# Moving the gates of a fused kernel out of its first twelve steps and spreading the conversion of its weights more evenly

## The chip, the cores and the metric

The kernel runs on one core of one Trainium2 chip. The metric is the device time of one execution in microseconds (us). Before the change the median is 494.94 us over four runs (490.22 to 495.63). All times inside a trace are microseconds from the start of its span; a timed run is about 1.8 us longer than its span.

## The reference

Two blocks follow each other. A gated linear attention recurrence runs over 768 positions of 4 × 8 heads of 48 values. Its output, laid out as 3072 rows of 384, goes through a multiplicative feed-forward network.

```python
# q, k, v, alpha: (4, 8, 768, 48) float32
for t in range(S):
    state = alpha[:, :, t, :, None] * state + np.einsum('bhd,bhe->bhde', k[:, :, t], v[:, :, t])
    y[:, :, t] = np.einsum('bhd,bhde->bhe', q[:, :, t], state)
x = y.transpose(0, 2, 1, 3).reshape(3072, 384)
a = x @ w1            # 384 x 1024
b = x @ w2
h = a * b @ w3        # 1024 x 1024
out = h @ w_out       # 1024 x 384
```

The four weights arrive as float64. The chip reads them as pairs of 32-bit words and converts them itself.

## The kernel before

The 3072 positions are cut into N = 24 chunks of 128; three chunks form one of eight groups. The kernel has three parts.

- **Part 1** is a loop over the chunks that does the recurrence; I call one pass a step. A step loads alpha, k, q and v a few chunks ahead (192 KB each, in rows of 48 floats), computes scores, a state and the result of the chunk before, and stores that result for its group.
- **Gates** are the products x @ w1 and x @ w2 of one group and one 128-column tile. They are done to full float32 accuracy in three parts. Half a gate, nine matmuls, is a *piece*. Pieces of the first groups are strewn into part 1 to fill TensorE's pauses.
- **Conversion** turns the raw 64-bit weights into three float32r parts. Each of the 12 tiles of w1 and w2 takes four *conversion steps*, which call VectorE and ScalarE; tiles are loaded up to three ahead.

Part 2 does the remaining gates, the conversion of w_out and w3 and eight folds w3 @ w_out. The final projection follows, 24 chunks.

```python
LATE = 10      # from this chunk on, the decays' sum uses two fp32r matmuls in place of one fp32

def convert(steps, ahead=3):
    for _ in range(steps):
        while weights and len(begun) < ahead:
            begun.append(weights.popleft())
            next(begun[-1])                       # issues the load of the raw tile
        if not begun:
            return
        ...                                       # one more step of the oldest tile

def load_gates(kk, c0, n):
    w = yield from to_fp32(None, ...)             # load; then 2 ScalarE, 5 VectorE instructions in 2 steps
    ...
    nc.scalar.activation(h, w, AF.Copy, ...)
    yield
    nc.vector.scalar_tensor_tensor(l, ...)
    nc.vector.scalar_tensor_tensor(m, ...)
```

The loop of part 1, with the places where gates and conversions are called:

```python
    convert(1, 1)                                 # ahead of the loop
    ...
    begin = {4 + 4 * g: (g, range(FH if g < 4 else KF)) for g in range(5)}

    for n in range(N + 1):
        store()                                   # the chunk's result, two transfers
        load_v(n + AHEAD - 1)
        load_a(n + 5)
        load_kq(n + AHEAD)
        if n:
            attend_state(n - 1)                   # L358
        if n < N:
            scores(n)                             # L339
        transposed(n + 1)                         # L299
        if n - 2 in begin:
            g, tiles = begin[n - 2]
            split_x(g, 0)                         # L385 to L387
            fill.extend(gate(g, f) for f in tiles)
        pieces = (0, 3, 3, 2)[(n - 6) % 4] if n > 5 else 0
        ...
        early = n < 7
        convert(1, 2 if n == 0 else 3)
        advance(n)
        if n:
            attend(n - 1)                         # L364
        outer(n)                                  # L311
        run(pieces > 0)                           # one piece
        if early:
            convert(1)
        decayed(n + 2)                            # L277: k and q times the decays
        logs(n + 4)                               # L246: logarithm of alpha
        if n in begin:
            load_x(begin[n][0])
        convert(early and n > 2)
        run(pieces > 1)
        decays(n + 3)                             # L261, or L264 from LATE on
        convert(early or n % 3 == 0)
        run(pieces > 2)
    store()
    ...
    todo, order = list(fill), []                  # part 2
    visits = [(g, range(FH, KF)) for g in range(4)] + [(g, range(KF)) for g in range(len(begin), NG)]
```

## Time and profile before

| view of the profile | value before | how to read it |
|---|---|---|
| span | 492.8 us | first to last instruction of the profiled run |
| PE (TensorE) busy | 462.0 us, 94% | nearly the whole span; ends of matmuls are modelled |
| DVE (VectorE) busy | 371.0 us, 75% | an average over stages with very different limits |
| ACT (ScalarE) busy | 250.1 us, 51% | |
| DMA queue q1 | 62.7% of 16 engines' span | again an average |
| chain that ended last | PE 73%, DVE 9%, DMA 8% | shares of the span |

The averages say that TensorE is the bound.

### The profile page before, as it was taken

To read this page: it belongs to the slowest core of one execution; us is meant where nothing else is said; L and a number is where in the kernel's file an instruction comes from. 1 tells how busy PE (TensorE), PEld (TensorE's weight loads), DVE (VectorE), ACT (ScalarE), POOL (GpSimd) and SP (SyncE) were. 2 spreads that over 40 slices of the span, in tenths; PEclk is the share of its full clock that TensorE was granted. 3 is DMA by queue.
4 is the path that set the end of the run, shared out by engine and by line. 5 is a ranking of instruction groups with operands and counts; after the bars stand their busy time and mean duration, and the time that the engine had idled before them with its cause. 6 is when DMAs were issued, how large, how long until landed. Compare 5 with 4: busy or idle time off the path is not lost.

```text
span 492.8 us, 9909 instructions
## 1 busy us (share of the span) xinstructions
PE 462.0 (94%) x3760; PEld 422.5 (86%) x3760; DVE 371.0 (75%) x620; ACT 250.1 (51%) x479; POOL 37.5 (8%) x83
## 2 busy tenths in 40 slices
PE   3788689999998979999999999999999999999997
PEld 1566479888998968999999988888888999999996
DVE  2779899887988684999999769686433786667771
ACT  2767677676765563555556444444222533333330
POOL 2132132021103100000000000000000000000000
PEclk9989999999999998999999999999999999999999
DMA  9999999899999963666454433320001875555511
GB/s 176 185 200 205 236 199 201 217 183 234 194 227 189 214 207 101 175 183 195 158 195 155 156 117 118 118 92 32 33 32 61 229 225 176 177 176 178 176 49 48
DMA packets 160495, 79.10 MB, mean 161 GB/s; under 512 B 104640, under 2 KB 154304, under 8 KB 160448
## 3 DMA queue, kind: packets, MB, share of 16 engines
q1 hardware_dynamic: 159168, 78.40, 62.7%
q0 software_dynamic: 1280, 0.08, 0.4%
q8 instruction: 29, 0.48, 0.4%
q14 instruction: 18, 0.15, 0.1%
HBM read 56.40 MB, written 22.06 MB: 159 GB/s over the span
## 4 chain that ended last, share of the span: by engine, by line
PE 73%; DVE 9%; DMA 8%; SPq 4%; issue 3%; ACT 2%; POOL 0%; DVEq 0%; POOLq 0%; ACTq 0%
PE bank L396 37%; PE bank L400 18%; PE bank L445 8%; DMA raw<-in_moe_w_dram 3%; PE bank L339 2%; PE bank L364 2%; DVE ms L342 2%; PE bank L439 1%; DMA xT<-xd 1%; DMA abd<-ab 1%; DMA dec<-ends 1%; PE bank L299 1%; SPq L130 1%; DVE qk L277 1%; SPq L124 1%
## 5 line engine op out<-in xcount | busy, mean ns | idle before, releaser
L396 PE MATMUL bank<-x,w 128*128 128x384 f32 x768 | 159.3, 341 | 0.0
L396 PEld LDWEIGHTS bank<-x,w 128*128 128x128 f32 x768 | 134.6, 188 | 3.5 <-issue 0.5
L398 ACT ACTIVATE t<-bank 128x384 f32<-128x384 f32 x152 | 74.5, 492 | 109.7 <-PE bank L396 97.8
L401 DVE SCALAR_TENSOR_TENSOR r<-bank,t 128x384 f32<-128x384 f32 x128 | 69.7, 555 | 34.0 <-ACT t L398 32.1
L400 PE MATMUL bank<-x,w 128*128 128x384 f32 x384 | 87.3, 335 | 0.4 <-DVE x L387 0.4
L396 PE MATMUL bank<-w3o,ab 128*128 128x384 f32 x384 | 70.4, 334 | 0.0
L400 PEld LDWEIGHTS bank<-x,w 128*128 128x128 f32 x384 | 68.3, 188 | 0.7 <-issue 0.7
L396 PEld LDWEIGHTS bank<-w3o,ab 128*128 128x128 f32 x384 | 66.9, 188 | 0.0
L445 PE MATMUL bank<-wo,w3T 128*128 128x384 f32 x128 | 42.6, 486 | 0.0
L189 ACT ACTIVATE rest<-raw 128x512 f32<-128x512 uint32 (+1 forms) x36 | 23.4, 651 | 33.0 <-DMA raw<-in_moe_w_dram 20.5
L412 DVE TENSOR_TENSOR ab<-r 128x384 f32<-128x384 f32 x64 | 35.6, 556 | 2.3 <-DMA abd<-ab 1.5
L400 PE MATMUL bank<-w3o,ab 128*128 128x384 f32 x192 | 37.1, 334 | 0.0
L445 PEld LDWEIGHTS bank<-wo,w3T 128*128 128x128 f32 x128 | 24.2, 189 | 14.9
L464 DVE TENSOR_TENSOR ab<-abl,ab 128x1024 fp32r<-128x1024 f32 x24 | 29.4, 1224 | 9.2 <-ACT ab L463 9.2
L339 PEld LDWEIGHTS bank<-qkT 48*128 48x128 f32 x384 | 25.4, 200 | 12.4 <-ACT qkT L301 5.7
L339 PE MATMUL bank<-qkT 48*128 48x128 f32 x384 | 30.3, 299 | 6.0 <-ACT qkT L301 4.3
L463 ACT ACTIVATE ab<-abl 128x1024 fp32r<-128x1024 f32 x24 | 25.5, 1064 | 19.0 <-PE bank L400 18.8
L400 PEld LDWEIGHTS bank<-w3o,ab 128*128 128x128 f32 x192 | 33.6, 188 | 0.0
L342 DVE TENSOR_TENSOR ms<-bank,keep 128x512 int32<-128x512 int32 x48 | 31.1, 684 | 1.7 <-PE bank L339 1.7
L194 ACT ACTIVATE power<-power,rebias 128x512 uint32<-128x512 uint32 (+1 forms) x36 | 25.3, 705 | 12.2 <-DVE power L193 12.2
L401 DVE SCALAR_TENSOR_TENSOR o<-bank,t 128x384 f32<-128x384 f32 x24 | 13.4, 557 | 22.4 <-issue 13.7
L277 DVE TENSOR_TENSOR qk<-kq,e 128x768 f32<-128x768 f32 x24 | 22.9, 953 | 9.5 <-ACT e L268 7.2
(69 smaller groups left out, 540.1 us busy)
## 6 DMA issues: line engine op xcount, KB each, us to landing
abd<-ab SPq DMA_DIRECT2D x64, 192.0 KB, 2.7
abl<-abd SPq DMA_DIRECT2D x24, 512.0 KB, 4.5
raw<-in_moe_w_dram SPq DMA_DIRECT2D x16, 512.0 KB, 3.9
xT<-xd SPq DMA_DIRECT2D x12, 576.0 KB, 4.2
raw<-in_moe_w_dram SPq DMA_DIRECT2D x24, 256.0 KB, 4.8
ac<-in_alpha_dram SPq DMA_DIRECT2D x24, 192.0 KB, 5.0
kq<-in_k_dram SPq DMA_DIRECT2D x24, 192.0 KB, 5.4
kq<-in_q_dram SPq DMA_DIRECT2D x24, 192.0 KB, 4.3
```

Of the source, the lines that this page charges most:

```text
L194: nc.scalar.activation(power, power, AF.Relu, scale=2.0 ** 23, bias=rebias)
L277: nc.vector.tensor_mul(qks[n % 3][:, :, :, 0:D], st.pop(("kq", n)), st.pop(("e", n)).rearrange("p i (h d) -> p i h d", h=H))
L339: nc.tensor.matmul(sc[i][:, j, :], qkT[r, 0, j, :], qkT[r, 1, j, :], start=True, stop=True)
L342: nc.vector.tensor_tensor(ms[:, i].bitcast(I32), sc[i].bitcast(I32), keep_bc, op=ALU.bitwise_and)
L396: nc.tensor.matmul(p1, w[part][i], x[part][i], start=(part == i == 0), stop=(part == 1 and i == n - 1))
L398: nc.scalar.activation(t, p1, AF.Copy, scale=(1.0 + 1.0 / P) * scale)
L400: nc.tensor.matmul(p2, w[2][i], x[2][i], start=(i == 0), stop=(i == n - 1))
L401: nc.vector.scalar_tensor_tensor(to, p2, -scale, t, op0=ALU.mult, op1=ALU.add)
L412: nc.vector.tensor_mul(ab, *r)
L445: nc.tensor.matmul(po, w3T[:, j, :], wo[:, j, :], start=(j == 0), stop=(j == KF - 1))
L463: nc.scalar.activation(t[:, 0], ab, AF.Copy, scale=1.0 - 2.0 ** -13)
L464: nc.vector.tensor_sub(t[:, 1], ab, t[:, 0].bitcast(FP32))
```

## The change

The intent: the first twelve steps lose their gates, and every step calls two conversion steps, so that VectorE and TensorE have less to do early on and the steps get shorter. At most two weight tiles are under way, not three. The eleven pieces that had been strewn there go to part 2. From step 12 on the same 24 pieces as before are done, now those of the groups 0 to 2; x of group 3 is only split, in step 24.

```diff
-    LATE = 10
+    LATE = 16
...
-    convert(1, 1)
...
-    begin = {4 + 4 * g: (g, range(FH if g < 4 else KF)) for g in range(5)}
+    begin = {10 + 4 * g: (g, range(FH if g < 3 else KF)) for g in range(4)}
...
-        pieces = (0, 3, 3, 2)[(n - 6) % 4] if n > 5 else 0
+        pieces = (0, 3, 3, 2)[n % 4] if n >= 12 else 0
...
-        early = n < 7
-        convert(1, 2 if n == 0 else 3)
+        convert(1, 2)
...
-        if early:
-            convert(1)
+        convert(1, 2)
...
-        convert(early and n > 2)
...
-        convert(early or n % 3 == 0)
...
-    visits = [(g, range(FH, KF)) for g in range(4)] + [(g, range(KF)) for g in range(len(begin), NG)]
+    visits = [(g, range(FH, KF)) for g in range(3)] + [(g, range(KF)) for g in range(len(begin), NG)]
```

Before step 12 this makes 24 conversion steps where there were 32, one of them ahead of the loop. "Halved" below means the first seven steps: 14 conversion steps where there were 25 in the loop. Steps 7 to 11 have more than before, 10 where there were 6.

## The prediction

> **What bounds the kernel now.** I read the 40 slices first, to see which engine is full where; then the busy time stage by stage; then the order of time of TensorE and of the SP queue, to price single pieces. Times are microseconds from the span's start. The slices:
>
> ```profile
> PE   3788689999998979999999999999999999999997
> DVE  2779899887988684999999769686433786667771
> PEclk9989999999999998999999999999999999999999
> DMA  9999999899999963666454433320001875555511
> ```
>
> One slice is 12.3 us. TensorE is full from the sixth slice on, but for the slice near 185; before that VectorE and the DMA engines are the full ones, and the DMA engines stay full until about 185, where the part with the recurrence (part 1) ends. I found the borders of the steps from the score matmuls (L339, one burst per step): step 0 starts at 15.1, step 7 at 58.0, step 12 at 100.3, and the last recurrence matmuls (L364, chunk 23) end at 195.5. The busy time of these stages:
>
> ```profile
> core 0: us, PE busy (x) PEld busy (x) DVE busy (x) ACT busy (x) POOL busy (x), PEclk, DMA share, GB/s
> 15.00:58.00 43.00, 35.26 (x512) 27.90 (x512) 36.53 (x64) 30.02 (x65) 10.23 (x20) 0.92 1.05 201
> 58.00:100.30 42.30, 39.37 (x495) 35.25 (x494) 39.91 (x69) 30.12 (x65) 9.29 (x14) 1.00 0.98 213
> 100.30:195.50 95.20, 89.35 (x1131) 81.34 (x1131) 72.75 (x126) 57.35 (x129) 14.47 (x30) 0.98 0.87 196
> 195.50:389.30 193.80, 193.80 (x1033) 176.53 (x1032) 148.81 (x280) 92.18 (x169) 0.00 (x0) 1.00 0.39 125
> 389.30:492.80 103.50, 99.83 (x576) 99.50 (x575) 68.95 (x73) 35.24 (x46) 0.00 (x0) 1.00 0.51 154
> ```
>
> Rows: steps 0 to 6, which have no gates; steps 7 to 11, with gates; the rest of part 1; gates and folds alone; the final projection. TensorE never pauses in the fourth row. So anything moved there costs its whole TensorE time, and anything gained must come from the 30 us or so in which TensorE waits in the first three rows and before them.
>
> Two prices from the order of time, TensorE first, then the SP queue at the start, when nothing but input loads is under way:
>
> ```profile
> 198.68 1.20 PE L396 MATMUL bank<-x,w 128*128 128x384 f32 x6
> 199.72 0.68 PE L400 MATMUL bank<-x,w 128*128 128x384 f32 x3
> 200.24 1.03 PE L396 MATMUL bank<-x,w 128*128 128x384 f32 x5
> ...
> 2.68 0.87 SPq L124 DMA_DIRECT2D ac<-in_alpha_dram  x1
> 3.60 0.83 SPq L136 DMA_DIRECT2D v<-in_v_dram  x1
> 4.47 0.92 SPq L130 DMA_DIRECT2D kq<-in_k_dram  x1
> 5.43 1.00 SPq L131 DMA_DIRECT2D kq<-in_q_dram  x1
> 6.48 1.10 SPq L124 DMA_DIRECT2D ac<-in_alpha_dram  x1
> 7.62 1.49 SPq L181 DMA_DIRECT2D raw<-in_moe_w_dram  x2
> ```
>
> Half a gate (nine matmuls, one "piece") takes 200.24 - 198.68 = 1.56. A 192 KB load of alpha, k, q or v takes the queue about 0.94 (mean of the five), one weight tile in two halves about 1.5; the two stores of a chunk's result took 0.86 (later in the same view). I take these issue times as the rate at which the full DMA engines accept work.
>
> **What the Trainium skill says.** "Trace Analysis", Identifying the Most-Contended Engine: matmul busy time is a poor measure, as matmuls are pipelined. The trace agrees: one gate matmul is shown with a mean of 341 ns, but nine take 1.56, 173 ns each; I count by pitch. "DMA: Bandwidth & Descriptors", Specifications: runs of 512 B or more are needed for line rate. A row of a head here is 48 floats, 192 B, and the trace fits: 201 GB/s at a share of 1.05 in part 1, but 229 GB/s at a share of only eight tenths in the slice near 388 that loads 512 B rows. "TensorE: Matmul & The Clock Gate", Part 1, puts the clock at half after an idle window. The trace agrees: after TensorE stood 2.16 for the state of step 3, sixteen L364 matmuls took 1.90 at 35.9 and 1.02 at 41.9. The same page (Architectural detail) says that VectorE and ScalarE are strict FIFOs; so a conversion that stands ahead of a mask delays it:
>
> ```profile
> 181.41 0.44 PE L358 MATMUL bank<-qkT,T 48*64 48x128 f32 x4
> 183.29 0.65 PE L358 MATMUL bank<-qkT,T 48*64 48x128 f32 x12 [1.45 <-DVE ms L342]
> ```
>
> Here the mask stood behind a split of x (L386, 1.35).
>
> **The change, part by part.**
>
> *Gates moved.* Before, pieces run in the pattern 0, 3, 3, 2 from step 6 to step 24: 3+3+2+0+3 = 11 before step 12, 24 in steps 12 to 23, 3 in step 24. After: none before step 12, 8+8+8 = 24 in steps 12 to 23, none in step 24. The gates and folds after part 1 then take, before, 93 pieces (3, and 45 gates) x 1.56 = 145.1, plus eight folds of 6.06 (12.30 from fold to fold less two gates) = 48.5: 193.6, which is the 193.8 of the fourth row. After: 52 gates = 104 pieces x 1.56 = 162.2, plus 48.5 = 210.7. That is +17.2, all of it on the path. The projection stays at 103.5. So the new span is E + 210.7 + 103.5 = E + 314.2, where E is the end of part 1, and it breaks even with 492.8 at E = 178.6: part 1 has to give 16.9 of its 195.5.
>
> *Conversions halved.* One weight takes four convert steps and, by pitch, about 3.7 of VectorE (two at 0.34, five at 0.60). Before: 26 convert steps in steps 0 to 6, 0.93 weight a step, so 3.4 of VectorE, beside 2.34 for the recurrence itself (two masks at 0.60, decay product 0.87, state 0.27): 5.8 against the 6.1 that such a step lasted. After: two convert steps a step, 1.84, sum 4.2. VectorE stops being the bound of the early steps. TensorE needs 4.5 (steps 1 and 4 lasted that: 21.44 to 25.95, 40.28 to 44.78).
>
> *DMA in the early steps.* A step asks for four loads (3.8), two stores (0.86) and half a weight (0.75): 5.4, more than TensorE or VectorE. So the DMA engines set these steps. For the scores of step 12, what was issued up to about step 9 must have landed: 54 loads x 0.94 = 50.8, eight chunks' stores 6.9, seven weights 10.5; 68.2 from about 3.0, so 71 at the earliest. The same count for step 7 of the kernel before is 34 loads, three stores, seven weights = 45.1, due at 48, while step 7 came at 58.0: a stretch of 55.0/45.1 = 1.22. With that stretch step 12 comes at 86. I choose half of the stretch, 1.13, and 80: a part of it came from weight loads that stood in the SP queue for buffers VectorE had still to read, and with two weights under way and three raw buffers this goes. So 20 us of the 100.3, of which 17.2 are the moved pieces and some 3 a true gain.
>
> *LATE from 10 to 16.* Six chunks lose a ScalarE copy (0.51) and a VectorE subtraction (0.56), and trade two matmuls of 0.17 for an fp32 one of 0.85: about 3 us of TensorE in all, in steps that the DMA engines bound, so hidden.
>
> *Steps 12 to 24.* The same 24 pieces, so 95.2 as before, plus what the delayed conversions do: 24 convert steps where there were 16, 8 x 0.92 = 7.4 of VectorE, which goes from 72.75 to some 80 of 95. A split (about 2.55) falls in steps without pieces, in which VectorE then has 2.34 + 1.84 + 0.47 + 2.55 = 7.2 against TensorE's 4.3. Waits for the mask, 0.9 to 1.5 long, already stand at three of these steps; each grows by some 0.6. With step 24's split ahead of its first gate I put the sum at 3.
>
> *One xT load and split less* (11 for 12), outside the tight stages: nothing.
>
> Sum: E = 80 + 95.2 + 3 = 178.2; span 178.2 + 314.2 = 492.4 against 492.8. A timed run is 1.8 longer than the span (494.63 for 492.8): 494.2.
>
> **Rivals.** (1) *VectorE alone bounds the early steps.* Then they fall to TensorE's 4.5 to 4.7, step 12 starts at 15 + 12 x 4.7 = 71, and the time is 485. For it: VectorE is the full row between 36 and 84, and two early steps did last 4.5. Against it: the DMA share is about 1 there as well, and those two steps drew on loads already made. (2) *DMA bounds all of part 1.* The bytes hardly fall (seven ab stores and one xT load less), step 12 comes at 86 or later, steps 12 to 24 hold more weight loads, and the moved pieces are nearly pure loss: 499 to 506. For it: the share of 0.87 in the third row. Against: TensorE is busy for 89 of 95 there. (3) *VectorE becomes the bound in steps 12 to 24*, with conversions, gates and splits together: 5 to 8 more, about 500.
>
> **Range and chances.** The rivals lie at 485 and 506 on both sides of a central case that nearly cancels, so the 2% limits (485 and 505) need a rival in full. 486 to 503; faster 0.08, same 0.80, slower 0.12.
>
> **What would show it.** Right: step 12's scores at 78 to 84; a DMA share near 1 and VectorE at some seven tenths before it; part 1 ending near 178; 211 between that and the projection, with TensorE unbroken. Wrong: step 12 before 75 (the DMA floor is no floor) or after 87; part 1's second half much longer than 98, with TensorE waiting for masks; half-clock stretches of more than 7 us in the early steps.

## The result, and the profile after

| | runs | median us | range |
|---|---|---|---|
| before | 4 | 494.94 | 490.22 to 495.63 |
| after | 4 | 509.27 | 506.57 to 511.57 |

The ratio is 1.031, with a 95% interval of 1.023 to 1.039: slower. A ratio here is the mean time of one kernel's fast runs over the mean of the other's fast runs of the same rounds, so it is not quite the ratio of the medians. The prediction was 494.2, with a range of 486 to 503; the time lies above it.

The slices of the kernel after; one slice is 12.6 us:

```profile
PE   3978686899899999999999999999999999999997
DVE  2498666678988989999997677873349467777761
PEclk9989899779899999999999999999999999999999
DMA  9999999999997555656552253200057235655511
```

VectorE's slices from the fifth to the eighth fell from 8 or 9 tenths to 6, as intended. The DMA engines are still full there. TensorE's clock, which the kernel before held at nine tenths, falls to seven at the eighth and ninth slice.

The stages of the kernel after, cut at the scores of step 12, at the end of the last recurrence matmuls and at the projection. The columns are those of the same view in the prediction (the stage and its length, busy time of each engine with its instructions, clock, share of the DMA engines, GB/s):

```profile
13.06:88.62 75.56, 60.89 (x906) 47.31 (x906) 53.23 (x89) 46.56 (x103) 19.63 (x34) 0.91 1.06 195
88.62:187.20 98.58, 93.73 (x1134) 84.60 (x1130) 82.05 (x145) 62.12 (x136) 17.85 (x30) 0.93 0.86 200
187.20:401.30 214.10, 211.89 (x1132) 193.66 (x1131) 165.39 (x304) 97.99 (x182) 0.00 (x0) 1.00 0.42 131
401.30:504.80 103.50, 99.75 (x576) 99.43 (x574) 64.11 (x68) 34.12 (x45) 0.00 (x0) 1.00 0.44 135
```

In the first stage no engine is full: TensorE 60.9 of 75.6, VectorE 53.2. Only the share of the DMA engines is at 1. Side by side with the kernel before and with what the prediction said:

| us | before | after | change | predicted after |
|---|---|---|---|---|
| scores of step 0 at | 15.1 | 13.1 | −2.0 | |
| scores of step 12 at | 100.3 | 88.6 | −11.7 | 80 |
| from there to the end of part 1 | 95.2 | 98.6 | +3.4 | 98.2 |
| from there to the projection | 193.8 | 214.1 | +20.3 | 210.7 |
| projection | 103.5 | 103.5 | 0 | 103.5 |
| span | 492.8 | 504.8 | +12.0 | 492.4 |

The last column misses by 8.6, 0.4 and 3.4. Most of the 3.4 shows in TensorE's order of time at the start of part 2 (start, duration, engine, line, and in brackets how long it was idle before and what it waited for):

```profile
187.65 0.79 PE L396 MATMUL bank<-x,w 128*128 128x384 f32 x3 [0.42 <-ACT x L385]
189.14 0.79 PE L396 MATMUL bank<-x,w 128*128 128x384 f32 x3 [0.69 <-DVE x L386]
190.50 0.76 PE L400 MATMUL bank<-x,w 128*128 128x384 f32 x3 [0.57 <-DVE x L387]
```

Part 2 now begins with a group whose split has only just been issued, in step 24. Its first gate waits for the three instructions of the split one after another. The second half of that gate begins at 191.10, 3.9 after the end of part 1; at its full pitch, 1.56, it would have begun at 188.8. That is 2.3 of the 3.4; the other 1.1 is spread over the part. In the kernel before, the last split of part 1 was issued in step 22 (VectorE's part began at 181.28), so that x was ready for the pieces at the start of part 2.

In the first stage TensorE waits, and the matmuls after a wait are slow as well:

```profile
58.87 1.65 PE L261 MATMUL bank<-la,after 128*128 128x384 f32 x2 [3.54 <-ACT la L246]
60.45 1.13 PE L358 MATMUL bank<-qkT,T 48*64 48x128 f32 x16
61.51 2.08 PE L339 MATMUL bank<-qkT 48*128 48x128 f32 x16
63.38 1.06 PE L299 MATMUL bank<-ident,qk 64*128 64x64 f32 x16
```

The sum of the decays waits 3.54 for the logarithm of alpha. The matmuls after it run at half rate: the scores take 2.08, where they take 1.16 later on. Summed from the start to 110 us (the longest stands ahead of step 0), the waits of TensorE for this logarithm (in total, how often, the longest) are in the kernel after

```profile
PE bank L261 <- ACT la L246: 14.3, 6, 4.5
```

and in the kernel before

```profile
PE bank L261 <- ACT la L246: 8.6, 4, 4.3
```

This suggested to me at first that alpha comes too late in the queue. The experiments tell otherwise.

### The profile page after: what moved, and what is told of

The parts are those of the page before. It is cut to its first block, busy times and chain, and to the rows that moved or that the text cites.

```text
span 504.8 us, 9918 instructions
## 1 busy us (share of the span) xinstructions
PE 470.6 (93%) x3760; PEld 427.0 (85%) x3760; DVE 367.4 (73%) x612; ACT 245.4 (49%) x472; POOL 41.0 (8%) x83
## 4 chain that ended last, share of the span: by engine, by line
PE 56%; DVE 3%; DMA 2%; issue 1%; ACT 0%; DVEq 0%; ACTq 0%
PE bank L396 32%; PE bank L400 16%; PE bank L445 6%; DMA raw<-in_moe_w_dram 2%; PE bank L439 1%; DVE r L401 1%; DVE w L199 0%; DVE ab L412 0%; DVE power L193 0%; DVE power L197 0%; DVE x L387 0%; DVE mant L196 0%; ACT t L398 0%; ACT rest L189 0%; DVE mant L190 0%
## 5 line engine op out<-in xcount | busy, mean ns | idle before, releaser
L396 PE MATMUL bank<-x,w 128*128 128x384 f32 x768 | 161.3, 344 | 3.4 <-ACT x L385 2.3
L396 PEld LDWEIGHTS bank<-x,w 128*128 128x128 f32 x768 | 136.2, 191 | 7.7 <-ACT x L385 2.7
L398 ACT ACTIVATE t<-bank 128x384 f32<-128x384 f32 x152 | 74.1, 491 | 119.1 <-PE bank L396 104.7
L400 PE MATMUL bank<-x,w 128*128 128x384 f32 x384 | 88.5, 338 | 0.8 <-DVE x L387 0.6
L400 PEld LDWEIGHTS bank<-x,w 128*128 128x128 f32 x384 | 69.0, 190 | 1.9 <-PE bank L396 1.4
L189 ACT ACTIVATE rest<-raw 128x512 f32<-128x512 uint32 (+1 forms) x36 | 23.3, 650 | 31.0 <-DMA raw<-in_moe_w_dram 25.6
L400 PE MATMUL bank<-w3o,ab 128*128 128x384 f32 x192 | 37.1, 334 | 0.0
L463 ACT ACTIVATE ab<-abl 128x1024 fp32r<-128x1024 f32 x24 | 25.5, 1062 | 18.8 <-PE bank L400 18.8
L301 ACT COPY qkT<-bank 128x512 f32<-128x512 f32 x48 | 26.0, 586 | 17.3 <-PE bank L299 17.3
L339 PEld LDWEIGHTS bank<-qkT 48*128 48x128 f32 x384 | 26.5, 210 | 7.5 <-ACT qkT L301 2.3
L401 DVE SCALAR_TENSOR_TENSOR o<-bank,t 128x384 f32<-128x384 f32 x24 | 13.4, 558 | 26.2 <-issue 15.2
```

The source lines that it names most:

```text
L301: nc.scalar.copy(qkT[:, :, :, ds(DP * half, DP)], tp[half])
L339: nc.tensor.matmul(sc[i][:, j, :], qkT[r, 0, j, :], qkT[r, 1, j, :], start=True, stop=True)
L396: nc.tensor.matmul(p1, w[part][i], x[part][i], start=(part == i == 0), stop=(part == 1 and i == n - 1))
L398: nc.scalar.activation(t, p1, AF.Copy, scale=(1.0 + 1.0 / P) * scale)
L400: nc.tensor.matmul(p2, w[2][i], x[2][i], start=(i == 0), stop=(i == n - 1))
L401: nc.vector.scalar_tensor_tensor(to, p2, -scale, t, op0=ALU.mult, op1=ALU.add)
```

## The experiments

The theories under test were these.

- **A, arrival.** The transfers together set the first twelve steps, with the gates or without them.
- **L, lateness of alpha.** Not their sum but their order: alpha, or the logarithm that is made of it, comes too late, and TensorE waits for it.
- **C, conversion.** The conversion's instructions stand ahead of the recurrence's own on VectorE and ScalarE; in one form of this theory, ahead of the logarithm. The expectations also name a wider form **V**: VectorE and ScalarE, with the conversions, set these steps.

Each kernel of the table was profiled and timed in three rounds against the kernel before on the same chip; the exception is the loads alone, which had one look. "To 12" is from the scores of step 0 to those of step 12, "second half" from there to the end of part 1, "rest" from there to the projection. "Wrong" marks kernels that give a wrong result on purpose. All runs were fast ones but one of e13. The ratios of e5, e13 and e18 leave out the first, profiled run; this matters for e13 alone.

| kernel | to 12 | second half | rest | span | ratio to before (95%) |
|---|---|---|---|---|---|
| before | 85.2 | 95.2 | 193.8 | 492.8 | 1 |
| after | 75.6 | 98.6 | 214.1 | 504.8 | 1.031 (1.023 to 1.039) |
| e1: before, gates moved alone | 86.2 | 92.1 | 212.4 | 509.1 | 1.039 (1.034 to 1.044) |
| e2: after, LATE = 10 | 78.9 | 98.0 | 213.3 | 506.8 | 1.037 (1.031 to 1.042) |
| e3: after without loads of v (wrong) | 64.0 | 96.0 | 212.1 | 488.6 | 0.994 (0.989 to 1.000) |
| e4: after, alpha one step earlier | 76.5 | 106.6 | 212.7 | 512.3 | 1.039 (1.032 to 1.046) |
| e5: before without loads of v (wrong) | 85.8 | 94.7 | 193.9 | 493.6 | 1.012 (1.007 to 1.016) |
| e7: after, conversions without loads (wrong) | 66.2 | 88.6 | 212.8 | 485.9 | 0.994 (0.990 to 0.998) |
| e8: after, loads without conversions (wrong) | 69.0 | 93.1 | 214.6 | 492.4 | 1.010 (1.005 to 1.015) |
| e9: e4 and the logarithm earlier | 74.1 | 104.2 | 213.7 | 508.5 | 1.040 (1.036 to 1.044) |
| e11: gates from step 8 on | 89.7 | 86.6 | 200.1 | 493.0 | 1.004 (1.000 to 1.009) |
| e13: after with useless matmuls | 80.4 | 90.3 | 212.4 | 499.8 | 1.030 (1.023 to 1.036), with a slow run; see below |
| e15: before without the first conversion | 92.3 | 92.0 | 193.8 | 494.4 | 1.000 (0.994 to 1.007) |
| e16: before, loads without conversions (wrong) | 84.1 | 91.9 | 193.7 | 485.3 | 0.987 (0.982 to 0.993) |
| e17: e1 without loads of v (wrong) | 74.3 | 94.2 | 212.2 | 498.8 | 1.017 (1.013 to 1.021) |
| e18: after, neither loads nor conversions (wrong) | 60.4 | 91.0 | 212.4 | 480.4 | 0.981 (0.974 to 0.987) |

One profile stands behind each of the four middle columns. e15 shows how far such columns can move by themselves: it differs from the kernel before by one conversion step ahead of the loop and takes the same time, but its "to 12" is 7.1 longer and its second half 3.2 shorter. So differences of a few microseconds between the stages of two single profiles mean little. The five steps 7 to 11 repeat better: 42.3 in the kernel before, 43.2 in e15. The ratios rest on three or four runs each.

### The gates moved alone (e1)

```diff
 (the kernel before)
-    begin = {4 + 4 * g: (g, range(FH if g < 4 else KF)) for g in range(5)}
+    begin = {10 + 4 * g: (g, range(FH if g < 3 else KF)) for g in range(4)}
-        pieces = (0, 3, 3, 2)[(n - 6) % 4] if n > 5 else 0
+        pieces = (0, 3, 3, 2)[n % 4] if n >= 12 else 0
-    visits = [(g, range(FH, KF)) for g in range(4)] + ...
+    visits = [(g, range(FH, KF)) for g in range(3)] + ...
```

> The kernel before with the gates alone moved as in the change; conversions (up to four steps a step) and LATE stay as before. Theory A: the early steps are as long as before (6.1 each up to step 6) or longer, since the weights come sooner; step 12 at 86 to 92, time 505 to 511, as in the changed kernel. Theory V: VectorE is fuller early, so step 12 comes later than in the changed kernel by 5 us or more, and the time is 513 or more.

Moving the gates alone takes eleven pieces, 17.2 us of TensorE, out of the steps 7 to 11. These five steps last as long as before. Step 12 comes at 101.1; A had said 86 to 92 and missed, and V had said 5 or more later than in the kernel after, which came true (the times that they had said, 505 to 511 and 513 or more, both missed 512.2 by about 1). e17 (below) tells the two apart. The stage of e1, which answers to the second row of stages in the prediction (42.30 long there, TensorE 39.37, share 0.98):

```profile
58.63:101.10 42.47, 32.86 (x395) 26.52 (x395) 29.13 (x49) 23.14 (x52) 6.53 (x13) 0.76 1.02 201
```

TensorE's work did not even fall by the whole 17.2, because its clock fell to 0.76: it waits more, and after the waits it runs at half rate. Part 2 pays for the pieces in full (193.8 to 212.4). So the move costs 16.3 of span (509.1 against 492.8). In the single profiles the rest of the change gives 4.3 of that back (504.8); the intervals of the two ratios overlap (1.034 to 1.044, 1.023 to 1.039), so the timed runs do not show it.

### The loads without v, with the gates in place and without (e3, e5, e17)

These three kernels use old values of v after the fifth chunk, which takes one transfer in four away from the inputs.

```diff
 (in load_v; e3: the kernel after; e5: before; e17: e1)
             st["v", n] = vs[n % len(vs)]
+            if n >= len(vs):
+                return
             nc.sync.dma_start(out=st["v", n][:, :, 0:D], in_=rows(v, n))
```

> The changed kernel without the loads of v from chunk 5 on (old v is used, a wrong result on purpose): a quarter of the input packets gone, nothing else. Theory A: about 1 us less for each step without gates, step 12's scores at 78 to 80 instead of 88.6, and 8 to 11 us less in all, so 498 to 501. Theory L: alpha waits fall only in part, 2 to 4 us less. Theory V: within 1 us of the changed kernel.

> The kernel before without the loads of v from chunk 5 on (a wrong result on purpose), as counterpart of the same edit of the changed kernel, which fell to 490.1, by 19 us. If TensorE bounds the kernel before from step 7 on, it gains little: 3 to 7 us, 488 to 492, about as long as the changed kernel without v, so that the change costs nothing once the loads are lighter. If transfers pace all of part 1 in both, it gains as much, 15 us or more, and ends below 480.

> The kernel with the gates alone moved, without the loads of v from chunk 5 on (a wrong result on purpose). If transfers hold its step 12 at 101.1, it comes at 88 to 94 and the time falls by 9 us or more, as it did in the changed kernel (11.6 earlier). If the conversions' arithmetic holds it, step 12 stays at 97 to 101, as in the kernel before without v.

In the kernel after, this takes 11.6 off the first twelve steps and 16 off the span, more than A had said. In the kernel before it takes nothing (85.8 against 85.2; the ratio is even 1.012, which I cannot explain, and both my forecasts of a gain missed). In e1 it brings step 12 from 101.1 to 89.0, as A had it and V had not. With e1 and e17 this makes a square for the steps 7 to 11:

| steps 7 to 11, us | with loads of v | without |
|---|---|---|
| with the eleven pieces | 42.3 (before) | 44.5 (e5) |
| without them | 42.5 (e1) | 31.4 (e17) |

Either alone saves nothing; both together save 11. The ratios of whole runs agree: 1, 1.012, 1.039 and 1.017 for before, e5, e1 and e17, by which leaving out v gains 2% only where the pieces are gone. The two stages without v, e5 and then e17:

```profile
56.97:101.47 44.50, 40.40 (x494) 36.29 (x493) 43.84 (x76) 33.22 (x73) 9.59 (x16) 0.96 0.90 204
```

```profile
57.57:88.98 31.41, 26.30 (x396) 21.64 (x395) 28.86 (x51) 23.10 (x52) 9.37 (x15) 0.89 1.01 211
```

In e5 the DMA engines have room (0.90), and TensorE and VectorE are full (40.4 and 43.8 of 44.5). In the kernel before, engines and transfers were both full in the same 42 us. This is what refutes the saving that I had expected: two bounds of the same length stood beside each other, and the change took away one. Whether the bound among the engines was TensorE or VectorE, the square does not tell; the pieces use both.

### Useless matmuls in the place of the gates (e13)

If TensorE has that much room in the steps 7 to 11 of the kernel after, then work put there must cost nothing. This kernel does eleven fillers of 14 matmuls each there, in the pattern of the old pieces.

```diff
 (the kernel after)
+    def filler(pieces):
+        for _ in range(pieces):
+            b = bank()[:, 0:2 * C]
+            for i in range(14):
+                nc.tensor.matmul(b, sums[:, 1], sums.rearrange("p i c -> p (i c)"), start=(i == 0), stop=(i == 13))
+        idle = (3, 3, 2, 0, 3)[n - 7] if 7 <= n < 12 else 0
         run(pieces > 0)
+        filler(idle > 0)
         (and in the same way after the two other run lines)
```

> The changed kernel with eleven pieces of useless matmuls (14 of 128 x 256 each, some 1.5 a piece, results dropped) in steps 7 to 11, where the kernel before has its eleven pieces: 17 us more work for TensorE. If the account is right that TensorE has this time to spare in the early steps, step 12 comes within 4 us of the changed kernel's 88.6 (perhaps earlier, as TensorE stays at full clock) and the time within 4 us of the changed kernel. If a step without gates is bound by TensorE, as my prediction had it for the saving of 17.2, the time rises by 12 to 17 us.

```profile
13.15:93.58 80.43, 77.11 (x1061) 64.99 (x1061) 55.04 (x93) 48.49 (x108) 19.34 (x34) 0.98 1.10 208
93.58:183.89 90.31, 86.98 (x1135) 79.35 (x1131) 80.89 (x144) 60.86 (x132) 16.90 (x29) 1.00 0.83 197
```

TensorE's busy time to step 12 grows from 60.9 to 77.1. The time does not: three runs have a mean of 504.7 against 493.0 for the kernel before in the same rounds, a ratio of 1.024, and the ratio 1.030 takes in the slow run in place of the profiled one; the kernel after has 1.031. Step 12 comes 5.0 later, a little more than the 4 that I allowed. The second half is 8.3 shorter, with a clock of 1.00 where the kernel after has 0.93. In the steps 7 to 11 TensorE is now busy without a pause (40.64 of 40.64, where the kernel after takes 36.9), so there the fillers cost 3.7. Over the whole kernel the 16 us cost nothing. That the higher clock of the second half pays for the rest is an inference from the two clocks, not tested apart.

### The gates from step 8 on (e11)

Between the two kernels lies one that keeps some gates early.

```diff
 (the kernel after)
-    LATE = 16
+    LATE = 12
-    begin = {10 + 4 * g: (g, range(FH if g < 3 else KF)) for g in range(4)}
+    begin = {6 + 4 * g: (g, range(FH if g < 4 else KF)) for g in range(5)}
-        pieces = (0, 3, 3, 2)[n % 4] if n >= 12 else 0
+        pieces = (0, 3, 3, 2)[n % 4] if n >= 8 else 0
-        convert(1, 2)
+        convert(1, 3)
-        convert(1, 2)
+        convert(n < 8)
         decays(n + 3)
+        convert(n < 8 or n % 2 == 1)
-    visits = [(g, range(FH, KF)) for g in range(3)] + ...
+    visits = [(g, range(FH, KF)) for g in range(4)] + ...
```

> Between the two kernels: gates from the ninth step on (32 pieces in part 1, eight of them before step 12, against 38 and 24), three convert steps a step up to step 7, then one and a half, LATE 12. If hidden pieces are what counts, 96 pieces remain after part 1: 149.8 + 48.5 + about 3 for the split = 201, and with the end of part 1 at 189 to 195 (between 187.2 and the 193.2 of the run with the gates alone moved) the span is 493 to 500 and the time 495 to 502, so nearer to the kernel before than to the changed one.

With eight pieces back in part 1, the rest takes 200.1 (96 pieces × 1.56 and 48.5 of folds make 198.3) and the span is 493.0: the same time as before, 1.004. Part 1 ends at 189.4, hardly later than in the kernel after (187.2). The eight pieces, 12.5 us of TensorE, cost part 1 some 2 us, with a few more conversion steps early on. The forecast of 493 to 500 for the span came true, at its edge.

### The loads by themselves (e6)

This kernel has nothing but transfers: twelve rounds of the loads v, alpha, k and q, then twelve rounds of the full mix of an early step, which has two stores of a chunk's result and half a weight more.

```python
for n in range(24):
    if n >= 12:
        ...                                # two stores, as in attend
    for name, src in (("v", v), ("a", alpha), ("k", k), ("q", q)):
        t = inp.tile([C, H, D], FP32, tag=name, name=name)
        nc.sync.dma_start(out=t, in_=rows(src, n))
    if n >= 12 and n % 2 == 0:
        ...                                # one weight tile, two transfers
```

> No arithmetic (a wrong result on purpose): twelve rounds of the four input loads of a chunk alone, then twelve rounds of four loads, two stores and half a weight, with four buffers each, and the output stores. Theory A (the transfers themselves pace the steps without gates): the second twelve take 72 to 76 us, 6.0 to 6.3 each, as long as the steps 0 to 11 of the changed kernel (75.6 us), and the first twelve some 4.0 to 4.5 each. Theory L (the engines could move more; what is late is the alpha load, through its place in the queue and its three buffers): the second twelve take my 5.4 each, 65 us, or less. Under theory V (VectorE and ScalarE with the conversions pace the steps) also 65 or less.

Three rows of the SP queue's order of time mark where the rounds begin and end, and two stages follow in the second fence (only the columns after the busy times count there: clock, DMA share, GB/s):

```profile
0.73 0.43 SPq L99 DMA_DIRECT2D v<-in_v_dram  x1
...
43.70 1.35 SPq L96 DMA_DIRECT2D xd<-x  x2
...
109.64 13.03 SPq L106 DMA_DIRECT2D out_dram<-o  x24
```

```profile
4.00:43.70 39.70, 0.00 (x0) 0.00 (x0) 1.00 1.10 216
43.70:109.60 65.90, 0.00 (x0) 0.00 (x0) 1.00 1.02 227
```

The loads alone take (43.70 − 0.73)/12 = 3.58 a round, the mix 65.9/12 = 5.49. My price was 3.8 and 5.4: the count of the prediction was right for transfers that have the chip to themselves. The steps of the kernel after are 6.3 (75.56/12), which is 15% longer. I had expected 6.0 to 6.3 here under A, and this missed; 65 us or less was what L and V had said. The rate differs to match: 227 GB/s alone, 195 in the kernel after, both at a share of 1. With that rate, 5.49 × 227/195 = 6.4, close to the 6.3 seen; this only says that the bytes are about the same, and is no cause. It also shows that a share of 1 does not mean that the engines can move no more. Why the same transfers are slower beside a working kernel, no run settles; e6 also lacks GpSimd's small transfers and writes v to closely packed rows.

### The weights' transfers and their conversion, apart (e7, e8, e16, e18)

In e7 the conversions read a tile that is always there, so that no weight of the gates is loaded. In e8 the weights are loaded, but the conversion is a copy of two values per partition, which releases the buffer, and GpSimd fills w12 with a constant. e18 does neither. e16 is e8's edit on the kernel before.

```diff
 (e7, in to_fp32)
-        raw = rawp.tile([C, n], I64, tag="raw", name="raw")
-        for i, src in enumerate(srcs):
+        raw = fixed if dst is None else rawp.tile([C, n], I64, tag="raw", name="raw")
+        for i, src in enumerate(srcs if dst else ()):
 (e8 and e16, load_gates: the body; e18: without the lines marked *)
+        raw = rawp.tile(...)                                   *
+        ...dma_start(raw, moe_w1), dma_start(raw, moe_w2)      *
+        yield
+        nc.vector.tensor_copy(out=seen, in_=words[:, :, 0])    *
+        yield
+        yield
+        nc.gpsimd.memset(h.bitcast(FP32), 0.5)
+        yield
+        nc.gpsimd.memset(l.bitcast(FP32), 0.5)
+        nc.gpsimd.memset(m.bitcast(FP32), 0.5)
```

> The opposite of the last: the conversions stay with all their instructions, but read one fixed tile, and the gate weights are not loaded (a wrong result on purpose): 12.6 of part 1's transfers' time by my 1.5 per two halves (8 weights before step 12) are gone. Theory A: step 12 at 76 to 79, and some 12 us less in all. Theory C with the weights' lateness as its root: the same. Theory C with VectorE's and ScalarE's work as its root: step 12 stays at 85 to 89.

> The changed kernel with the gate weights still loaded but not converted (GpSimd fills the converted weights with a constant, a wrong result on purpose): all transfers stay, the conversions leave VectorE and ScalarE. Theory C (a step without gates is a chain through the in-order ScalarE and VectorE: the logarithm that TensorE's next matmul needs stands behind a conversion, which stands behind its weights): step 12 comes at 76 to 81 instead of 88.6. Theory A (transfers pace it): step 12 stays at 86 to 89. Either way the second half of part 1 gets a little shorter too.

> The changed kernel with neither the gate weights' loads nor their conversion (constants from GpSimd, a wrong result on purpose). The first twelve steps then have TensorE's 4.5, VectorE's 2.3 and transfers of 3.6 (measured alone) plus the stores' 0.9. If loads and conversions together made up the 6.3 of a step, step 12 comes at 68 to 74; if something else holds the steps (the round trip of the row sums through memory, the order of the recurrence), at 78 or later.

> The kernel before with its gate weights loaded but not converted (a constant from GpSimd, a wrong result on purpose). If the fast conversions' arithmetic holds step 12 at 100.3, it comes at 82 to 90 and the time falls by 8 to 15 us, with TensorE as the next bound (twelve steps of 4.5, 17.2 of gates and 15 of start are 86). If the transfers hold it, step 12 stays at 97 to 101.

The stage from step 0 to step 12 of e7, e8 and e18, in this order:

```profile
14.74:80.92 66.18, 57.33 (x906) 45.22 (x907) 64.45 (x117) 51.49 (x114) 21.50 (x34) 0.97 1.10 189
12.17:81.16 68.99, 59.19 (x907) 46.66 (x907) 30.73 (x53) 36.30 (x84) 28.72 (x62) 0.94 0.99 204
13.12:73.48 60.36, 57.82 (x907) 45.91 (x907) 30.40 (x47) 35.46 (x84) 29.85 (x61) 0.97 1.10 186
```

Against the kernel after, the first twelve steps lose 9.4 without the weights' loads, 6.6 without the arithmetic and 15.2 without both, down to 5.0 a step. e7's step 12, at 80.9, lies just beyond the 76 to 79 of A; e8's, at 81.2, lies at the edge of C's 76 to 81 and not in A's 86 to 89; e18's 73.5 is within its range. So the conversions are not hidden behind the transfers as the prediction had it; both take part, and the transfers have the larger share (the ratios of e7 and e8, 0.994 and 1.010, have intervals that do not meet). In e8 the bytes of the kernel after move at 204 GB/s in place of 195. In the kernel before, the arithmetic's removal leaves the twelve steps almost as they were (84.1; its first step alone took 12.2, where it took 6.3 before, and the other eleven are 7.0 shorter) and saves 7.5 of span, 3.0 of it before the scores of step 0. Its step 12, at 96.2, is just below the 97 to 101 of the transfers.

The twelve steps are not all alike. Cut at the scores of step 7:

| us | steps 0 to 6 | steps 7 to 11 |
|---|---|---|
| before | 42.9 | 42.3 |
| e1: gates moved alone | 43.7 | 42.5 |
| after | 38.7 | 36.9 |
| e3: after without loads of v | 37.9 | 26.1 |
| e7: after without loads of weights | 38.3 | 27.8 |
| e8: after without arithmetic | 36.5 | 32.5 |
| e18: after without either | 37.1 | 23.3 |

Whatever is taken from the kernel after, the first seven steps lose at most 2.2; the steps 7 to 11 lose up to 13.6. So A is shown for the steps 7 to 11. In the first seven TensorE is busy for 34.0 of 38.7, and the loads made ahead may carry them; what sets them is not shown.

One reading goes through all sixteen full kernels. From the scores of step 0 to those of step 12, the share of the DMA engines is never under 0.98 and the rate lies between 186 and 217 GB/s. Rate times time gives the bytes: 11.2 MB in 60.4 us in e18, 12.5 MB in 66.2 in e7, 14.7 MB in 75.6 in the kernel after, 17.6 MB in 85.2 in the kernel before, 19.7 MB in 92.3 in e15. These are bytes that happened to be moved, loads ahead included, so the row is no proof of a cause; with the square it fits A.

It also tells what halving the conversions did. From e1 to the kernel after, the bytes to step 12 fall from 17.6 to 14.7 MB, and those of the second half rise from 16.4 to 19.7. Three megabytes of transfers went from the one side of step 12 to the other: the SP queue issued 13 halves of weight tiles (0.26 MB each) up to there in place of 20, and the rest is mostly inputs loaded less far ahead. With it step 12 came 12.5 earlier, and the second half got 6.5 longer. No run halves the conversions alone; LATE and the conversion ahead of the loop changed as well between e1 and the kernel after (e2 and e15, below).

### Alpha and its logarithm earlier (e4, e9)

```diff
 (e4; the kernel after)
-            st["a", n] = inp.tile([C, H, D], FP32, tag="ac", name="ac")
+            st["a", n] = inp.tile([C, H, D], FP32, tag="ac", name="ac", bufs=4)
     load_a(4)
+    load_a(5)
-        load_a(n + 5)
+        load_a(n + 6)
 (e9: this, and the logarithm one step earlier)
-        logs(n + 4)
+        if n + 4 >= LATE:
+            logs(n + 4)
         decays(n + 3)
+        if n == 0:
+            logs(4)
+        if n + 5 < LATE:
+            logs(n + 5)
```

> The changed kernel with alpha loaded one step earlier, into a fourth buffer: the same bytes in another order. Theory L: the six waits of TensorE for the logarithm (14.3 us in all before step 13) go, step 12 comes near 80 and the time falls by 6 to 9 us. Theory A: the wait moves to k, q or v; step 12 stays within 2 us of 88.6 and the time within 2 us of the changed kernel.

> The changed kernel with alpha loaded and its logarithm taken one step earlier for the chunks under 16: the same work and bytes, but no logarithm that TensorE waits for stands behind this step's conversion. Theory C: the waits for the logarithm (14.3 us in six before step 13) fall to under 5, step 12 at 78 to 82, 5 to 9 us less in all. Theory A: the waits move to other inputs, step 12 within 2 us of 88.6, time within 3 us of the changed kernel.

The wait for the logarithm goes, but for the one at the start. It comes back under another name. TensorE's waits of e4 up to 110 us:

```profile
PE bank L299 <- DVE qk L277: 16.0, 8, 3.4
PE bank L261 <- ACT la L246: 4.4, 1, 4.4
```

The transposes now wait 16.0 for the product of k and q with the decays, where the kernel after had waited 14.3 for the logarithm; in e9 it is 17.7. Step 12 comes at 89.5 and 87.2, against 88.6. So L is refuted, and so is the form of C in which the logarithm stands behind the conversion. A rival is left. On ScalarE, which the prediction takes to be strictly in order, the conversion's first instruction (L189) waits until its weights land: from 13 to 89 us 5.7 in the kernel after, 7.9 in e4 and 13.0 in e9. What stands behind it would be held up as well. e7 takes away this wait together with the bytes, so it cannot tell the two apart, and no run moves the conversion away from a late weight. Both kernels are even slower than the kernel after, by 0.8 and 0.9% of the ratios, whose intervals overlap with its own, and the step with the first gates shows it: from step 13 to step 14 it is 14.6 in the kernel after, 19.0 and 18.3 here, 9.0 in e13.

### Two small parts (e2, e15)

```diff
 (e2; the kernel after)
-    LATE = 16
+    LATE = 10
 (e15; the kernel before)
-    convert(1, 1)
```

> The changed kernel with LATE back at 10 alone. Chunks 10 to 15 get the ScalarE copy (0.51) and the VectorE subtraction (0.56) again and spare TensorE about 0.5 each. Both theories: within 1% of the changed kernel; if ScalarE's and VectorE's order matters in the early steps, up to 3 us more.

> The kernel before without the conversion that stands ahead of the loop (the one part of the change that could help it): the first scores come at 13 instead of 15.1. As the early steps are bound by transfers and the conversions, not by the start, I expect 0 to 2 us less, within noise; a gain of 3 or more would make it a version better than both.

LATE = 10 gives 1.037 where the kernel after gives 1.031. The intervals overlap, so a gain of LATE = 16 of some half per cent is possible and not shown. The scores of step 0 come at 12.8 in e15 instead of 15.1, as they do at 13.1 in the kernel after. The time is the same, 1.000: the two microseconds at the start do not show in it, and step 12 of its profile comes at 105.1.

## Why the prediction was wrong

**The step that failed.** It is the last sentence of the part on the DMA in the early steps: "So 20 us of the 100.3, of which 17.2 are the moved pieces and some 3 a true gain." Step 12 was to come at 80 and came at 88.6. Two things are wrong in it, one in each half of the sum.

*The moved pieces give nothing back.* The sentence takes their TensorE time as time of the steps. The square shows 42.3 with them and 42.5 without: the transfers held these steps to the same length. The prediction had seen a DMA share of 0.98 in that very row of its stages, with TensorE at 39.4 and VectorE at 39.9 of 42.3, and still counted the pieces' TensorE time as time that the steps would lose. The whole gain of step 12 comes with the rest of the change, most likely the halved conversions: from e1 to the kernel after it is 12.5, not 3, and the second half pays 6.5 of it back. As an account of the 20 us the sentence is thus off both ways. The 80 itself came from the count of transfers, to which the second point belongs.

*The true gain was taken too small, and so was the stretch.* The count of 68.2 for the transfers from about 3.0 was right for transfers alone: e6 measures 5.49 for the mix that I had at 5.4. The kernel before stretched its count by 1.22, and I chose 1.13, for the reason that loads stuck in the queue would go. The kernel after stretched it by (88.6 − 3.0)/68.2 = 1.26. The reason was right in kind: up to step 12 the SP queue's own waits for buffers fell from 25.5 to 12.4 us, those of the weight loads from 3.6 to 0. But the transfers did not go faster for it; the rate was even lower, 195 GB/s against 207 in the kernel before. (Half of a stretch of 1.22 is also 1.11, not 1.13.) With the unreduced 1.22 the prediction would have been 86 for step 12, about 498 for the span and 500 for the time.

**A smaller miss.** "With step 24's split ahead of its first gate I put the sum at 3" put that split into part 1. It stands at the start of part 2, unhidden, and the part took 214.1 in place of 210.7. The second half came at 98.6 against 98.2 without it, so this wrong place cost 2.3 of the 3.4 that the part took more than said. That the second half fits to 0.4 is then in part luck: a share of the 3 was put there for a split that is not in it, and e13, with the same conversions and the same gates, has 90.3.

**What was right.** The price of the moved pieces in part 2 was +17.2 and all on the path; e1 alone shows 212.4 − 193.8 = 18.6, the split's wait included. The DMA share near 1 and VectorE at seven tenths before step 12 (53.2/75.6 = 0.70) came as said. The sign for a wrong prediction, step 12 after 87, came too. So did the half-clock stretches: the mean clock to step 12 is 0.91, where it was 0.96. By an estimate from these means that is (1 − 0.91)/0.5 × 75.6 = 14 us at half clock, where the sign asked for more than 7. A reading to put right: TensorE's order of time gives the two bursts of L364 as 1.97 (at 35.80) and 1.09 (at 41.87), not 1.90 and 1.02; the conclusion stays.

**The rivals.** The second one, that the DMA bounds all of part 1 and the moved pieces are nearly pure loss (499 to 506), came nearest, just under the measured 509.3. What I held against it, TensorE's 89 busy of 95 in the second half, was no argument for the first twelve steps. Rival 1 (VectorE alone, 485) is refuted by the kernel after itself: VectorE is at 0.70, the steps are 6.3, and step 12 came at 88.6 where that rival had 71. Rival 3 (VectorE fills the second half) had VectorE at 82.1 of 98.6, and the half grew by 3.4, as in the central case.

**What stays open.** Why the same transfers run at 227 GB/s alone and at 195 beside the kernel. How much of an early step is the conversion's arithmetic and how much its loads: 6.6 and 9.4 make 16.0, close to the 15.2 of both. Two bounds side by side would not add up like this; a chain from weight to conversion to recurrence could, and was not traced. What sets the first seven steps. And why the profiled runs of e4 and e9 lose 6 to 8 us in the second half; most of it is lost in their step with the first gates, and its cause was not traced.

## What to carry to other kernels

When two resources are both full in a stage, work taken from one saves nothing until the other has shrunk too; test it before the move by taking the other one's work away, and look at the square. Work that runs beside another full resource can be nearly free where it stands (eight pieces, 12.5 us, cost part 1 of e11 some 2) and be paid in full where it is moved to. And a stretch measured between counted and real transfer times should be kept as measured, unless a run shows that its cause goes.

## What the Trainium skill lacked or had wrong

- "DMA: Bandwidth & Descriptors", How a descriptor splits into AXI transactions (with the overhead of about three cycles for each packet in the section before it, Why small descriptors are slow): the page has the parts for a row of 192 bytes, but no rate for it. From its rules, rows at multiples of 192 bytes need 6, 12, 10 and 8 beats of 32 bytes, 9 in the mean, and 3 of overhead, for 6 of use; half of the page's ceiling of 435 GB/s is an estimate of 217. The loads of such rows alone ran at 216 GB/s. No run changed the alignment, so the agreement is no proof.
- No page gives a rate for such a mix of transfers beside a working kernel: 227 GB/s for the mix of an early step alone, 195 in the kernel after, both at a full share. Why they differ, no run settles.
- "TensorE: Matmul & The Clock Gate", Why this matters for your kernels, asks to avoid pauses of more than about 3 us. Here shorter ones were enough: in the kernel after, TensorE stood 2.20 ahead of the transposes at 133.87, these took 1.12 in place of 0.66, and the mean clock from 134.0 to 138.5 was 0.66.
- No page has numbers for useless matmuls put into TensorE's pauses: with those of e13, 16.2 us busy, the second half's clock was 1.00 in place of 0.93, and the time stayed the same within the noise.
